# Seven block products for eight in the last feature pairs, and half steps of the attention joined, in a chain of linear attention and two feature layers

## The chip, the core and the metric

The kernel runs on one core of one Trainium2 chip. The metric is the device time of one execution in microseconds; before the change the median of three runs is 912.08 us (911.79 to 914.33).

## What is computed

Linear attention with random features, and then two feature layers on its output, all in float32 or near it (the reference is numpy):

```python
q_p, k_p = (phi(q_s), phi(k_s))           # phi: exp(x @ omega.T - |x|^2/2 - max) / sqrt(m)
kv = np.einsum('bhsm,bhsd->bhmd', k_p, v)
z = np.sum(k_p, axis=2)
num = np.einsum('bhsm,bhmd->bhsd', q_p, kv)
den = np.einsum('bhsm,bhm->bhs', q_p, z)[..., None] + 1e-06
...
h = x @ w_in;  g = h * np.cos(h);  x = g @ w_out                   # first layer
h = x @ w_in;  g = h * np.clip(h + 3.0, 0.0, 6.0) / 6.0;  x = g @ w_out   # second layer
```

There are 4 x 576 = 2304 tokens, 8 heads of 64, 128 random features, a model width of 512 and a feature width of 2048.

## The kernel before

**Order.** The kernel writes down tasks with `add(name, key, engines, function, after, alloc, use)`: a key, a duration per engine, the tasks it comes after, and the ring of buffers it takes a place in. `Plan.order` goes through them with a clock of its own. Each engine that is free takes the ready task with the smallest key (plus the number that `BIAS` holds for its kind), and the instructions are issued in the order that comes out. So keys and durations set the order on each engine; the hardware waits only on the data. Where the plan foresees TensorE idle in the first stretch it puts in matmuls on zeros (`filler`, issued at L1272 and L1281).

**Attention.** 18 chunks of 128 tokens for the keys and 18 for the queries (`chunk`). Each chunk has a projection onto the features (L503, 64 rows of the array), in some chunks a second product for the squared norms (L512), maxima on VectorE (L529) and exponents on ScalarE (L555). Even and odd heads are the halves `hf` 0 and 1. A key chunk adds to the sums `kv` in two tasks, one per half (L570; 64 columns of the array); a query chunk is transposed (L600), divided into a numerator task `num` per half (L613, 64 columns), normalised (L634) and transposed back into `xx` (L648). In the trace each of these float32 matmuls is two records, so that half a numerator has 16.

**First layer, first 4 of 16 feature blocks.** `pair_slot`: plain products, with weights and inputs split into a rounded high part and the rest, three matmuls for one (high by high, low by high, high by low); the input product is L846, the output product L872, 256 columns each.

**The rest: sweeps of two feature pairs.** A pair is 256 features; there are 6 left of the first layer and 8 of the second, numbered j from 0 to 13. A sweep takes two pairs over three blocks of 768 tokens (2 x `NS`). For each pair and block, `quad` makes the first product h = x @ w_in by seven block products in place of eight (L1058), each of 6 matmuls of 384 columns. The seven use sums of blocks: sums of the input (t1 to t4, made in `forms`, kept in DRAM as `xd`) and of the weights (`pair_forms`). Each chain has the banks A, Bk, C, Dk, E. Product 0 goes to A; a seed (ScalarE, L1071) copies A to Bk while product 4 goes to E; then products 1 on A, 5 on Bk (giving u2), a seed of Bk to C, product 6 on Bk (u3), a seed of Bk to Dk, product 2 on C and product 3 on Dk. E is copied out (L401) and added to Bk and C (L1095, L1098).

In the second layer the gate is a ReLU on ScalarE (L1115) and a VectorE step (L1118); then the result is split into a high part (L401, ScalarE) and a low part (L408, VectorE or GpSimd). `units` makes the second product, g @ w_out, as eight plain outputs of 128 rows by 384 tokens, 12 matmuls each (L1196), evicted into `xx` by VectorE (L1223) and stored (L1241). The very last output is cut in two of 192 tokens. Quads have six PSUM banks (`hb`), outputs two (`yb`).

## Time and profile before

| | |
|---|---|
| median of 3 runs | 912.08 us (911.79 to 914.33) |
| the profiled execution | 912.33 us, its span 910.6 us |
| TensorE busy | 902.7 us (99%), 6970 matmuls |
| VectorE / ScalarE / GpSimd busy | 640.7 / 542.1 / 229.7 us |
| granted TensorE clock | 0.999 of full speed |
| matmuls of the second product in sweeps (L1196) | 2028 |

The span is from the first to the last instruction of the one profiled execution; the time of a run is a little longer. A matmul's mean duration in the tables includes its way through the array, which overlaps with the next one, so spacing is read from starts. An engine named as a releaser is the one whose semaphore came last.

### The profile page before, as it was taken

The page shows a single profiled execution, that of the slowest core. Times are in us where ns is not written, and L with a number is a line of the kernel's source. Part 1 is how long each engine was busy: PE and PEld are TensorE (multiplying, and loading weights), DVE is VectorE, ACT ScalarE, POOL GpSimd, SP SyncE. Part 2 cuts the span into 40 slices and gives each one's busy share as a digit, 9 for nine tenths or more (in the row PEclk, how much of TensorE's full clock was granted, in tenths as well). Part 3 has the DMA queues.
Part 4 walks back from the last instruction along what each step waited for, and adds up shares of the span by engine and source line. Part 5 has one row for each costly group of instructions (what it writes and reads, how often), then busy time and mean ns, then how long its engine had stood idle before and what let it go on. Part 6 is the DMA issues. An engine that isn't in the chain of part 4 may idle for free.

```text
span 910.6 us, 17402 instructions
## 1 busy us (share of the span) xinstructions
PE 902.7 (99%) x6970; PEld 882.8 (97%) x6970; DVE 640.7 (70%) x1038; ACT 542.1 (60%) x1084; POOL 229.7 (25%) x174
## 2 busy tenths in 40 slices
PE   9999999999999999999999999999999999999998
PEld 7888999999999999999999999999999999999998
DVE  4886896776679788977668789765676667745442
ACT  7988888985487656656456467654544344434320
POOL 2130313335445433322242433012022002200000
PEclk9999999999999999999999999999999999999999
DMA  8645353423678647741645167522932646153412
GB/s 318 217 143 171 130 196 141 165 73 97 228 298 278 222 144 260 271 174 52 238 136 199 47 254 324 196 93 97 391 136 93 242 157 226 47 199 112 192 54 103
DMA packets 44736, 162.02 MB, mean 178 GB/s; under 512 B 4592, under 2 KB 15984, under 8 KB 40560
## 3 DMA queue, kind: packets, MB, share of 16 engines
q1 hardware_dynamic: 44512, 160.85, 48.9%
q8 instruction: 55, 0.90, 0.4%
q14 instruction: 25, 0.20, 0.1%
q10 hardware_dynamic: 144, 0.07, 0.0%
HBM read 118.43 MB, written 42.47 MB: 177 GB/s over the span
## 4 chain that ended last, share of the span: by engine, by line
PE 95%; DVE 2%; issue 1%; DMA 1%; ACT 1%; SPq 0%; POOL 0%; DVEq 0%; ACTq 0%
PE b L1196 38%; PE b L1058 33%; PE b L846 6%; PE b L872 5%; PE b L503 4%; PE b L570 2%; PE b L613 2%; PE b L600 2%; PE b L512 1%; PE b L648 1%; DMA F<-kT 1%; DVE R L408 0%; PE b L1272 0%; DVE F L529 0%; DVE F L736 0%
## 5 line engine op out<-in xcount | busy, mean ns | idle before, releaser
L408 POOL TENSOR_TENSOR R<-F,R 128x384 fp32r<-128x384 f32 (+3 forms) x103 | 170.8, 1663 | 282.1 <-ACT R L401 248.3
L401 ACT ACTIVATE R<-F 128x768 fp32r<-128x768 f32 (+3 forms) x242 | 174.0, 739 | 101.5 <-PE b L1196 56.5
L1196 PE MATMUL b<-R,R 128*128 128x384 f32 (+1 forms) x1062 | 201.7, 334 | 0.0
L1196 PEld LDWEIGHTS b<-R,R 128*128 128x128 f32 x1062 | 185.1, 188 | 0.0
L1058 PE MATMUL b<-R,R 128*128 128x384 f32 x966 | 183.7, 334 | 0.0
L1196 PE MATMUL b<-R 128*128 128x384 f32 (+1 forms) x966 | 183.3, 334 | 0.0
L1058 PEld LDWEIGHTS b<-R,R 128*128 128x128 f32 x966 | 168.7, 188 | 0.0
L1196 PEld LDWEIGHTS b<-R 128*128 128x128 f32 x966 | 168.4, 188 | 0.0
L1058 PE MATMUL b<-R 128*128 128x384 f32 x798 | 152.8, 334 | 0.0
L1058 PEld LDWEIGHTS b<-R 128*128 128x128 f32 x798 | 139.4, 188 | 0.0
L408 DVE TENSOR_TENSOR R<-F,R 128x384 fp32r<-128x384 f32 (+3 forms) x147 | 128.3, 895 | 11.2 <-ACT R L401 9.2
L1223 DVE SCALAR_TENSOR_TENSOR F<-b,F 128x384 f32<-128x384 f32 (+1 forms) x133 | 73.4, 552 | 87.7 <-PE b L1196 86.8
L1071 ACT ACTIVATE b<-b 128x384 f32<-128x384 f32 x126 | 59.4, 477 | 78.0 <-PE b L1058 77.5
L555 ACT ACTIVATE F<-b,F 128x128 f32<-128x128 f32 x288 | 81.9, 411 | 11.0 <-DVE F L540 10.4
L938 POOL TENSOR_TENSOR F<-F 128x256 f32<-128x256 f32 x40 | 31.3, 797 | 194.7 <-DVE F L736 186.8
L401 ACT ACTIVATE F<-b 128x512 f32<-128x512 f32 (+2 forms) x104 | 55.6, 551 | 30.0 <-PE b L1058 16.1
L529 DVE TENSOR_REDUCE F<-b 128x4 f32<-128x512 f32 x72 | 47.9, 685 | 33.1 <-PE b L512 19.4
L846 PE MATMUL b<-R 128*128 128x256 f32 x432 | 62.1, 290 | 0.0
L872 PE MATMUL b<-R 128*128 128x256 f32 x432 | 58.5, 286 | 0.2 <-ACT F L888 0.2
L846 PEld LDWEIGHTS b<-R 128*128 128x128 f32 x432 | 54.5, 190 | 1.7
L872 PEld LDWEIGHTS b<-R 128*128 128x128 f32 x432 | 54.2, 191 | 0.9 <-ACT F L888 0.4
L503 PE MATMUL b<-F 64*128 64x128 f32 x576 | 42.8, 286 | 0.6 <-DMA F<-kT 0.6
(71 smaller groups left out, 917.2 us busy)
## 6 DMA issues: line engine op xcount, KB each, us to landing
R<-xd SPq DMA_DIRECT2D x77, 768.0 KB, 6.8
F<-w SPq DMA_DIRECT2D x32, 1024.0 KB, 5.3
xd<-R SPq DMA_DIRECT2D x42, 768.0 KB, 4.0
F<-vn SPq DMA_DIRECT2D x18, 260.0 KB, 4.2
F<-qT SPq DMA_DIRECT2D x18, 256.0 KB, 2.8
yy<-F SPq DMA_DIRECT2D x18, 256.0 KB, 2.2
F<-kT SPq DMA_DIRECT2D x17, 256.0 KB, 4.0
F<-qn SPq DMA_DIRECT2D x15, 256.0 KB, 3.8
```

The costliest lines, as they stand in the source:

```text
L401: nc.scalar.activation(out=o, in_=i, func=ACTF.Copy)
L408: (nc.gpsimd if e == "p" else nc.vector).tensor_tensor(out=o, in0=a, in1=b, op=ALU.subtract)
L503: nc.tensor.matmul(out=buf["pj", kind, c, o][:, 128 * i:128 * i + 128], lhsT=buf[X][64 * o:64 * o + 64, 128 * i:128 * i + 128], rhs=omd[64 ...
L529: nc.vector.tensor_reduce(out=buf[MX][:, o:o + 4], in_=pj, axis=AX.X, op=ALU.min)
L555: nc.scalar.activation(out=p[:, o], in_=pj[:, o], func=ACTF.Exp, scale=-1.0, bias=mx[:, b:b + 1])
L846: nc.tensor.matmul(out=o, lhsT=w[:, 128 * kc:128 * kc + 128], rhs=v, start=(kc == 0 and j == 0), stop=(kc == KC - 1 and j == 2), skip_grou ...
L872: nc.tensor.matmul(out=y, lhsT=w[:, o], rhs=v, start=(first and fi == 0 and j == 0 and ec % 2 == 0), stop=(last and fi == 1 and j == 2 and ...
L938: (nc.gpsimd if e == "p" else nc.vector).tensor_tensor(out=st[:, o:o + 256], in0=x, in1=y, op=op)
L1058: nc.tensor.matmul(out=o, lhsT=a, rhs=v, start=first and kc == 0 and q == 0, stop=kc == 1 and q == 2, skip_group_check=True)
L1071: nc.scalar.activation(out=buf[to][:, 0:NS], in_=buf[frm][:, 0:NS], func=ACTF.Copy)
L1196: nc.tensor.matmul(out=o, lhsT=a, rhs=v, start=q == 0 and not seeded, stop=q == 6 * SWEEP - 1, skip_group_check=seeded)
L1223: nc.vector.scalar_tensor_tensor(out=o, in0=y, scalar=r, in1=o if s else buf[YP].bitcast(F32), op0=ALU.mult, op1=ALU.add)
```

## The change

It does four things.

1. For the last two feature pairs (j = 12 and 13, the last sweep; `FAST` = 12) the second product is made by seven block products too (`fast_units`). Its blocks are 256 output rows by 384 tokens, over 128 features of each pair. The 256 rows are done 128 at a time, so each block of tokens has two chains (`e_` 0 and 1) of seven products, of 6 matmuls of 384 columns each (two pairs by three), in banks `fa` to `fe` out of all eight (`h8`). Four evictions per chain add A, Bk, C and Dk to the output, and E is added to two of the four outputs by evictions of its own (`ev0`). The weights' second half becomes seven forms (`wv`) where it had four blocks, and the gated result gets sums t1 to t4 of its own (`gated`: tiles `tt`, then high and low parts in the rings `gs` and `gt`). The last output is not cut in two any more, and each output is stored by itself.
2. The two halves of a key chunk's sums are one task, and so are the two halves of a query chunk's numerator.
3. An exponent of the first half waits for its own maximum alone, where the norms come from TensorE.
4. The plan counts 0.095 us for a change between 128-row, 64-row and 64-column work on TensorE (`T_TURN`), and all keys' constants (`T_P`, `T_LATE`, `BIAS` and others) and some choices of engine (`ENGS`) have other values, so that the order is another one throughout.

The core of the diff:

```diff
-T_P = 37.717
+T_P = 28.537
...
-T_LATE = 36.64
-T_ONE = -48.724
+T_LATE = 56.155
+T_ONE = 70.329
...
-T_K = 2.362
-T_Q = 32.71
+T_K = 2.456
+T_Q = 44.05
...
+FAST = sum(L_PAIRS) - SWEEP
...
+    **{f"wf{i}": spread(*at, 3584, 1) for i, at in enumerate([(R1, 8704), (R2, 0), (R1, 0)])},
+    **{f"wo{i}": spread(*at, 2048, 1) for i, at in enumerate([(R1, 12288), (R2, 3584), (R1, 3584)])},
+    **{f"wv{i}": spread(*at, 3584, 1) for i, at in enumerate([(R1, 12288), (R2, 3584)])},
+    "xf6": spread(R1, 5632, 1536, 2) + spread(R2, 7168, 1536, 4) + spread(R1, 0, 1536, 2),
+    "gs": spread(R1, 16384, 768, 4) + spread(R2, 13312, 768, 2) + spread(R1, 4608, 768, 1),
+    "gt": spread(R1, 19456, 1536, 2) + spread(R2, 14848, 1536, 1) + spread(R1, 3072, 1536, 1),
+    "wg": spread(F1, XX + 5888, 1536, 1) + spread(F1, XX, 1536, 1),
+    "tt": spread(F1, XX + 7424, 768, 1) + spread(F1, XX + 1536, 768, 2) + spread(F1, XX + 4096, 768, 1),
+    "h8": spread(PS, 4, 1, 2) + spread(PS, 0, 1, 4) + spread(PS, 6, 1, 2),
...
+RINGS["gsL"] = RINGS["gs"] + [(a, x, x + 768) for a, lo, hi in RINGS["xf6"] for x in (lo, lo + 768)]
+RINGS["gtL"] = RINGS["gt"] + RINGS["xf6"]
...
+T_TURN = 0.095
...
+                    if e == "t" and t.half not in (None, half):
+                        end, half = end + T_TURN, t.half
...
-        add(P1, k, {"t": 1.0}, proj, ["om"], alloc=pr, use=[X, P0])
+        add(P1, k, {"t": 0.9}, proj, ["om"], alloc=pr, use=[X, P0])
...
-            for hf in range(2):
-                E = ("e", kind, c, hf)
-                for b, r0, r1 in rows(c):
-                    def kv(e, b=b, r0=r0, r1=r1, hf=hf, E=E, first=not kv_parts[b, hf]):
-                        if first:
-                            bank(("kv", b, hf))
-                        p = buf["kv", b, hf]
+            E = [("e", kind, c, hf) for hf in range(2)]
+            for b, r0, r1 in rows(c):
+                first = not kv_parts[b]
+                K0, K1 = ("kv", b, 0), ("kv", b, 1)
+
+                def kv(e, b=b, r0=r0, r1=r1, first=first):
+                    if first:
+                        bank(("kv", b, 1))
+                    for hf in range(2):
                         for h in range(4):
                             for j in (0, 64):
                                 nc.tensor.matmul(
-                                    out=p[j:j + 64, 65 * h:65 * h + 65],
+                                    out=buf["kv", b, hf][j:j + 64, 65 * h:65 * h + 65],
+                                    lhsT=buf[E[hf]][r0:r1, 128 * h + j:128 * h + j + 64],
...
-                    parts = kv_parts[b, hf]
-                    name = ("kv", b, hf) if not parts else ("kv", b, hf, c)
...
-                    parts.append(name)
+                if first:
+                    add(K0, k + 2.9, {"t": 0.01}, lambda e, K0=K0: bank(K0), alloc="kv0", use=E + [V])
+                name = K1 if first else ("kv", b, 1, c)
+                add(name, k + 3, {"t": 0.96}, kv, kv_parts[b][-1:], alloc="kv1" if first else None, use=E + [V, K0] + ([] if first else [K1]))
+                kv_parts[b].append(name)
...
-            def num(e, QT=QT, NUM=NUM, hf=hf):
-                p = bank(NUM)
...
-            add(NUM, k + 4.5 + 0.1 * hf, {"t": 0.58}, num, [("kvs", b, hf) for b, _, _ in rows(c)] + ([("num", c, 0)] if hf else [("tp", c, 1)]), alloc="pt",
-                use=[QT] + [("kvs", b, 0) for b, _, _ in rows(c)])
+            def num(e):
+                bank(("num", c, 1))
+                for hf in range(2):
...
+            if hf == 0:
+                add(NUM, k + 4.5, {"t": 0.01}, lambda e, NUM=NUM: bank(NUM), [("tp", c, 1)], alloc="pt", use=[QT])
+            else:
+                add(NUM, k + 4.6, {"t": 0.96}, num, [("kvs", b, x) for b, _, _ in rows(c) for x in range(2)], alloc="pt",
+                    use=[("qt", c, 0), QT, ("num", c, 0)] + [("kvs", b, 0) for b, _, _ in rows(c)])
...
-    def pair_forms(j):
-        k = w_key(j) + 12.0
...
+    def seven(j, hf, ring):
...
-        made = split("a", WF, FORM_HI, 0, 768, lambda: buf[T0][:, 0:768], [T0], [("low", j, 0)], 0, "wf")
+        made = split("a", WF, 0, 768, lambda: buf[T][:, 0:768], [T], [("low", j, hf)], 0, ring)
...
-        made += split("c", ("wfh", j, "c"), FORM_HI, 768, 1024, lambda: buf[ST], [ST, WF], prev, 0.3)
-        return made, split("o", WO, 1024, 0, 1024, lambda: buf[T1], [T1], [("low", j, 1)], 12, "wo")
+        return made + split("c", (f + "h", j, "c"), 768, 1024, lambda: buf[ST], [ST, WF], prev, 0.3)
+    def pair_forms(j):
+        place = f"{j % 3}"
+        made = seven(j, 0, "wf" + place)
+        if j >= FAST:
+            return made, seven(j, 1, "wv" + place)
...
+            if j >= FAST:
+                gated(n, k, ((("b", A, c11, 5.2, 0, NS), ("r", HS, ("c12", n), 12.1, NS, NP), ("d", Dk, c21, 13.8, 3 * NS, NS))), s * n_p + n_p - 1 == tour.index((s, p)))
+                return
...
+        def gated(n, k, parts, final):
...
+                def relu(e, h=h, o=o, N=N, x=x):
+                    w = tile_of(W, [128, 4 * NS]) if x == "b" else buf[W]
+                    nc.scalar.activation(out=w[:, o:o + N], in_=buf[h][:, 0:N], func=ACTF.Relu, bias=3.0)
...
+                def gg(e, h=h, o=o, N=N):
+                    w = buf[W][:, o:o + N]
+                    nc.vector.scalar_tensor_tensor(out=w, in0=w, scalar=6.0, in1=buf[h][:, 0:N], op0=ALU.min, op1=ALU.mult)
...
+            def t13(e):
+                w = buf[W]
+                sub2(e, tile_of(T1, [128, NP]), w[:, NS:3 * NS], w[:, 0:2 * NS])
...
+            def t2(e):
+                sub2(e, tile_of(T2, [128, NP])[:, 0:NS], buf[W][:, 2 * NS:3 * NS], buf[T1][:, 0:NS])
...
+            def t4(e):
+                sub2(e, buf[T2][:, NS:NP], buf[W][:, 3 * NS:4 * NS], buf[T2][:, 0:NS])
...
+            add(T1, k + 13.0, {"v": 0.96}, t13, [("gg", n, "b"), ("gg", n, "r")], alloc="tt", use=[W])
+            add(T2, k + 13.5, {"v": 0.56}, t2, alloc="tt", use=[W, T1])
+            add(("tu", n), k + 14.5, {"v": 0.56}, t4, [("gg", n, "d")], use=[W, T2])
+            for x, src, o, N, ready, dk in (
+                ("b", W, 0, NS, ("gg", n, "b"), 6.2), ("c", W, 2 * NS, NS, ("gg", n, "r"), 13.0), (0, T1, 0, NP, T1, 13.7), ("d", W, 3 * NS, NS, ("gg", n, "d"), 14.6), (1, T2, 0, NP, ("tu", n), 15.0),
...
+                def hi(e, src=src, o=o, N=N, G=G):
+                    rnd(e, tile_of(G, [128, 2 * N])[:, 0:N], buf[src][:, o:o + N])
+
+                def lo(e, src=src, o=o, N=N, G=G):
+                    sub(e, buf[G][:, N:2 * N], buf[src][:, o:o + N], buf[G][:, 0:N].bitcast(F32))
+
+                add(G, k + dk, {"a": 0.82 if N == NP else 0.52}, hi, [ready] + ([last_g[0]] if last_g[0] else []), alloc=y + far, use=[src])
+                add((y + "l", n, x), k + dk + 0.5, {"v": 0.96 if N == NP else 0.56}, lo, use=[src, G])
+                last_g[0] = G
+
...
+        G_AT = {"b11": ("gs", "b", 0, NS), "b21": ("gs", "d", 0, NS), "b22": ("gs", "c", 0, NS),
+                "t1": ("gt", 0, 0, NP), "t3": ("gt", 0, NS, NP + NS), "t2": ("gt", 1, 0, NP), "t4": ("gt", 1, NS, NP + NS)}
...
+        def fast_units(k_, s, p):
...
+            for e_ in range(2):
...
+                def product(i, bank_of, first, after, alloc=None, e_=e_, k=k, m=m):
...
+                        for q in range(SWEEP):
+                            wv, g = buf["wv", SWEEP * s + q], buf[G[q]]
+                            c0 = 256 * w + 128 * e_
+                            for t, (a, v) in enumerate(((c0, hi), (FORM_HI + c0, hi), (c0, lo))):
+                                nc.tensor.matmul(out=o, lhsT=wv[:, a:a + 128], rhs=g[:, v:v + NS], start=first and q == 0 and t == 0,
+                                                 stop=q == SWEEP - 1 and t == 2, skip_group_check=True)
...
+                    name = bank_of if alloc else ("fp", m, i)
+                    add(name, k + 2.1 * ORDER.index(i), {"t": 1.04}, fn, [(y + "l", n0 + q, z) for q in range(SWEEP)] + [f for q in range(SWEEP) for f in made[SWEEP * s + q][1]] + list(after),
+                        alloc=alloc, use=G + [("wv", SWEEP * s + q) for q in range(SWEEP)] + ([] if alloc else [bank_of]))
...
+                def seed(to, frm, dk, after, k=k):
+                    def fn(e):
+                        bank(to)
+                        nc.scalar.activation(out=buf[to][:, 0:NS], in_=buf[frm][:, 0:NS], func=ACTF.Copy)
+
+                    add(to, k + dk - 10, {"a": 0.5}, fn, after, alloc="h8", use=[frm])
+
+                head = e_ == 0 and p == tour[s * n_p][1]
+                gate = [("ba", n0 + SWEEP - 1)] + ([("y2",) + tour[k_ - 1] + (7,)] if head else [("fa", m - 1)]) + ([("fd", m - 2)] if m - 2 >= 2 * s * n_p else [])
+                product(0, A, True, gate, "h8")
+                seed(Bk, A, 1.1, [A] + ([] if head else [("fd", m - 1)]))
+                product(4, E, True, [A], "h8")
+                c11 = product(1, A, False, [Bk, E])
+                u2 = product(5, Bk, False, [c11])
+                seed(C, Bk, 7.4, [u2])
+                u3 = product(6, Bk, False, [C, u2])
+                seed(Dk, Bk, 9.6, [u3])
+                c12 = product(2, C, False, [u3])
+                c21 = product(3, Dk, False, [c12])
...
+                for u, own, done, dk in ((e_, A, c11, 6.0), (6 + e_, Bk, Dk, 11.0), (4 + e_, C, c12, 12.8), (2 + e_, Dk, c21, 14.9)):
...
+                    def ev(e, b=own, ec=ec, tok=tok):
+                        o = xx[:, ec, tok]
+                        nc.vector.scalar_tensor_tensor(out=o, in0=buf[b][:, 0:NS], scalar=r, in1=o, op0=ALU.mult, op1=ALU.add)
+
+                    def ev0(e, ec=ec, tok=tok, E=E):
+                        o = xx[:, ec, tok]
+                        nc.vector.scalar_tensor_tensor(out=o, in0=buf[E][:, 0:NS], scalar=r, in1=o, op0=ALU.mult, op1=ALU.add)
+
+                    def st(e, ec=ec, tok=tok):
+                        nc.sync.dma_start(out=out[128 * ec:128 * ec + 128, tok], in_=xx[:, ec, tok])
...
+                    if c:
+                        add(("ev0", s, p, u), k + 4.0, {"v": 0.56}, ev0, old, use=[E])
+                        old = [("ev0", s, p, u)]
+                    add(("ev2", s, p, u), k + dk, {"v": 0.56}, ev, [done] + old, use=[own])
+                    add(("st2", p, u), k + dk + 0.5, {"d": 0.4}, st, [("ev2", s, p, u)])
...
-            units(k_, s, p)
+            (fast_units if SWEEP * s >= FAST else units)(k_, s, p)
...
-def _pairs(w_in, w_out, first):
+def _pairs(w_in, w_out, first, fast=0):
...
-    parts = [a[:, 0, 0], a[:, 0, 1], a[:, 1, 1], a[:, 1, 0], o[:, 0], o[:, 1]]
-    return np.ascontiguousarray(np.concatenate(parts, axis=2)[first:]).view(np.uint64)
+    o = [o[:, 0, :, 0:256], o[:, 0, :, 256:512], o[:, 1, :, 0:256], o[:, 1, :, 256:512]]
+    parts = [a[:, 0, 0], a[:, 0, 1], a[:, 1, 1], a[:, 1, 0]]
+    all_ = np.concatenate(parts + o, axis=2)
+    if fast:
+        all_[-fast:] = np.concatenate(parts + [o[0], o[2], o[3], o[1]], axis=2)[-fast:]
+    return np.ascontiguousarray(all_[first:]).view(np.uint64)
...
-        "w2": _pairs(inputs["moe2_w_in"], inputs["moe2_w_out"], 0),
+        "w2": _pairs(inputs["moe2_w_in"], inputs["moe2_w_out"], 0, SWEEP),
```

## Rows read from the trace of the kernel before

**Rows 1.** The page's table of engines: busy time, share of the span, instructions.

```profile
PE 902.7 (99%) x6970; PEld 882.8 (97%) x6970; DVE 640.7 (70%) x1038; ACT 542.1 (60%) x1084; POOL 229.7 (25%) x174
```

**Rows 2.** What TensorE waited for: us in all, times, longest; five in all.

```profile
PE b L648 <- DVE F L634: 2.6, 3, 1.6
...
PE b L872 <- ACT F L888: 0.2, 1, 0.2
```

**Rows 3.** Stretches (from:to, us): busy time of each engine, granted clock, DMA share, GB/s.

```profile
40.00:60.00 20.00, 19.25 (x344) 17.04 (x344) 17.51 (x34) 18.41 (x54) 6.73 (x6) 1.00 0.34 110
...
120.00:140.00 20.00, 20.00 (x226) 18.52 (x226) 17.78 (x41) 17.24 (x36) 4.68 (x4) 1.00 0.50 172
...
300.00:400.00 100.00, 100.00 (x579) 100.00 (x578) 84.06 (x126) 60.55 (x103) 34.71 (x22) 1.00 0.61 217
...
844.00:878.00 34.00, 34.00 (x198) 34.00 (x197) 15.96 (x27) 11.32 (x22) 0.00 (x0) 1.00 0.35 137
```

**Rows 4.** Groups by line and shape: count, busy us, mean ns of one, idle before.

```profile
L401 ACT ACTIVATE R<-F 128x768 fp32r<-128x768 f32 x98 | 81.4, 842 | 33.3 <-PE b L1196 19.1 <-DVE F L1022 8.3 <-DVE F L1148 2.2
L1223 DVE SCALAR_TENSOR_TENSOR F<-b,F 128x384 f32<-128x384 f32 x131 | 72.7, 555 | 86.0 <-PE b L1196 85.1
...
L1118 DVE SCALAR_TENSOR_TENSOR F<-F 128x768 f32<-128x768 f32 x24 | 23.5, 977 | 16.0 <-ACT F L1115 15.9
...
L1272 PE MATMUL b<-F 128*128 128x128 f32 x26 | 4.7, 299 | 0.0
...
L1281 PE MATMUL b<-F 128*128 128x128 f32 x14 | 2.1, 290 | 0.0
```

**Rows 5.** The chain that ended last, in order of time: start us, us, what.

```profile
225.46 2.88 PE b L846 x24
...
419.27 14.56 PE b L1058 x84
```

**Rows 6.** Timeline of the end, all engines: start us, us, engine, line, operation.

```profile
904.79 0.81 PE L1196 MATMUL b<-R 128*128 128x192 f32 x6
...
906.78 0.83 PE L1196 MATMUL b<-R,R 128*128 128x192 f32 x6
907.65 0.36 DVE L1223 SCALAR_TENSOR_TENSOR F<-b,F 128x192 f32<-128x192 f32 x1 [0.98 <-PE b L1196]
```

**Rows 7.** DMA issues of the output: count, KB each, median us to landing.

```profile
yT<-F SPq DMA_DIRECT2D x7, 192.0 KB, 1.9
...
yT<-F SPq DMA_DIRECT2D x2, 96.0 KB, 1.6
```

**Rows 8.** Timeline of one quad: two products, and the seed between them.

```profile
820.55 1.20 PE L1058 MATMUL b<-R 128*128 128x384 f32 x6
820.75 0.47 ACT L1071 ACTIVATE b<-b 128x384 f32<-128x384 f32 x1 [0.69 <-PE b L1058]
```

**Rows 9.** TensorE's timeline in the attention: start us, us, line, tile, count.

```profile
9.30 0.69 PE L570 MATMUL b<-F 128*64 128x65 f32 x16
...
13.12 1.16 PE L570 MATMUL b<-F 128*64 128x65 f32 x32
14.20 1.16 PE L503 MATMUL b<-F 64*128 64x128 f32 x16
...
88.50 0.69 PE L570 MATMUL b<-F 128*64 128x65 f32 x16
...
92.85 0.69 PE L613 MATMUL b<-F 128*64 128x65 f32 x16
93.47 1.70 PE L846 MATMUL b<-R 128*128 128x256 f32 x12
95.10 0.69 PE L613 MATMUL b<-F 128*64 128x65 f32 x16
...
217.71 0.69 PE L613 MATMUL b<-F 128*64 128x65 f32 x16
```

More of the change, by code (lines that the diff above doesn't have):

```diff
@@ L125, in phase @@
     n1 = L_PAIRS[0] * NT // NP
[L126 removed]
+    if x in ("ws", "wt", "clamp", "shift", "sign", "low", "wv", "wvh", "wvl", "wf", "wfh", "wfl", "st", "sum", "wo", "wol"):
         return 0 if name[1] < SWEEP else 1 if name[1] < L_PAIRS[0] else 2
@@ L154, in engines, with halved @@
     return {e: SLOW[kind][e] for e in ENGS.get(f"{kind}{x}", "v")}
-SHARED = ("clamp", "shift", "sign", "low", "wl", "xl", "gl", "wfl", "wol", "st", "sum", "ta", "tb", "xfl", "gl2")
+SHARED = ("clamp", "shift", "sign", "low", "wl", "xl", "gl", "wfl", "wol", "st", "sum", "ta", "tb", "xfl", "gl2", "wvl", "tt", "tu", "gsl", "gtl")
 def shares(name):
     return isinstance(name, tuple) and (name[0] in SHARED or name[0] in ("nr", "gg", "wk2") and name[2] == "r")
+def halved(name):
+    x = name[0] if isinstance(name, tuple) else name
+    if len(name) > 2 and (x == "pj" and not name[3] or x == "kv" and not name[2] or x == "num" and not name[2]):
+        return None
+    return 2 if x in ("kv", "num") else int(x in ("ps", "pj"))
 class Task:
@@ L171, in __init__ @@
         self.shares = shares(name)
+        self.half = halved(name)
 NEVER = 1e9
+T_TURN = 0.095
 class Plan:
@@ L224, in order @@
         lock = [0.0]
+        half = 0
         def can(t, now, e):
@@ L442, in attention_moe_moe2_kernel @@
     last_chunk = {b: ((b + 1) * S - 1) // 128 for b in range(B)}
-    kv_parts = {(b, hf): [] for b in range(B) for hf in range(2)}
+    kv_parts = {b: [] for b in range(B)}
     t_q = T_K * (NCH + N_EARLY)
@@ L761, in attention_moe_moe2_kernel, with pair_weight @@
     pairs = [(w1, i) for i in range(L_PAIRS[0])] + [(w2, i) for i in range(L_PAIRS[1])]
-    for j, (src, i) in enumerate(pairs):
+    def pair_weight(j, hf):
+        src, i = pairs[j]
         gate = [("ba", 3 * j - 5 - j % 2)] if j >= SWEEP else [("in", W_AFTER[j], 3)]
@@ L766, in attention_moe_moe2_kernel @@
                 gate.append(("tb", m, NT // NP - 1, "t4"))
+        weight(src[i, :, 2048 * hf:2048 * hf + 2048], (j, hf), w_key(j) + 12.0 * hf, gate, "ws2")
+    for j in range(FAST):
         for hf in range(2):
-            weight(src[i, :, 2048 * hf:2048 * hf + 2048], (j, hf), w_key(j) + 12.0 * hf, gate, "ws2")
+            pair_weight(j, hf)
+    for hf in range(2):
+        for j in range(FAST, len(pairs)):
+            pair_weight(j, hf)
     last_x = [None]
@@ L939, in sums, with hi, lo @@
             return fn
[L941 removed]
+        prev = [("low", j, hf)]
         for i in range(4):
[L943 to L944 removed]
+            name = ST if i == 0 else ("sum", j, i, hf)
+            add(name, k + 0.2 + 0.01 * i, engines("sum", phase(WF)), sums(i), prev, alloc=None if i else "st", use=[T] + ([ST] if i else []))
             prev = [name]
[L946 to L947 removed]
+        return made + split("c", (f + "h", j, "c"), 768, 1024, lambda: buf[ST], [ST, WF], prev, 0.3)
[4 more added lines that the diff above has]
+            return made, seven(j, 1, "wv" + place)
+        k = w_key(j) + 24.0
+        WO, T = ("wo", j), ("wt", j, 1)
+        def hi(e):
+            rnd(e, tile_of(WO, [128, 2048])[:, 0:1024], buf[T])
+        def lo(e):
+            sub(e, buf[WO][:, 1024:2048], buf[T], buf[WO][:, 0:1024].bitcast(F32))
+        add(WO, k, {"a": 1.03}, hi, [("low", j, 1)], alloc="wo" + place, use=[T])
+        add(("wol", j), k + 0.1, engines("wol", phase(("wf", j))), lo, use=[T, WO])
+        return made, [WO, ("wol", j)]
     def stage():
@@ L1267, in filler @@
     def filler(last):
-        for hf in range(2):
-            for b in range(B):
-                if last.get(("kv", b, hf)) and not last.get((kv_parts[b, hf][-1])):
-                    return lambda: nc.tensor.matmul(out=buf["kv", b, hf][:, 0:FILL], lhsT=zero[:, 0:128], rhs=zero[:, 0:FILL], start=False, stop=False, skip_group_check=True)
+        for b in range(B):
+                if last.get(("kv", b, 1)) and not last.get(kv_parts[b][-1]):
+                    return lambda: nc.tensor.matmul(out=buf["kv", b, 1][:, 0:FILL], lhsT=zero[:, 0:128], rhs=zero[:, 0:FILL], start=False, stop=False, skip_group_check=True)
         for b in range(N_A):
```

100 lines of the change are left out of this document (62 added, 38 removed).

## The prediction

> **What bounds the kernel.** I read the table of engines first. TensorE is busy in 99% of the 910.6 us span; no other engine passes 70% [rows 1]. A busy TensorE need not be a full one, so the list of its waits comes next: five waits in the whole execution, from 2.6 us in all for the attention's last transpose down to 0.2 us [rows 2]. The table of stretches then shows that this holds everywhere: from 120 to 140 us and from 300 to 400 us TensorE has no gap, at a granted clock of 1.00, the 2.4 GHz level, while VectorE and ScalarE are 61 to 89% busy [rows 3]. Only the first 90 us or so are looser: 19.25 of 20 us between 40 and 60, with ScalarE at 18.4 [rows 3], and part of that is matmuls on zeros (L1272 and L1281), which the plan puts where it foresees TensorE idle: 4.7 and 2.1 us [rows 4]. So the time is the sum of what TensorE does. A matmul taken away is a gain of its own spacing, unless it leaves a hole; work added on the other engines costs nothing until TensorE waits for it.
>
> The spacing comes from the chain of work in order of time. 84 matmuls of 384 columns take 14.56 us, 173.3 ns each, and 24 of 256 columns take 2.88 us, 120 ns each [rows 5].
> By the Trainium skill ("TensorE: Matmul & The Clock Gate", Back-to-back issue gap) a warm matmul of N columns takes N/2.4 + 2.5 ns, 162.5 ns here; the trace's 173.3 is 7% longer, and by the page term 1 below would be 5.85 us in place of 6.24, the whole sum 0.4 us smaller.
>
> **1. Seven products for eight: -6.24 us.** The last sweep has three token blocks. For each, the second product now takes 96 matmuls: 8 outputs of 12. After, two halves of 7 products of 2 pairs of 3 matmuls: 84. That is 36 matmuls fewer, times 173.3 ns. The sweep's first product is as before.
>
> **2. The last output is no longer cut in two: -0.1 us.** Now its 24 matmuls of 192 columns start at 904.79, and the last ends at 906.78 + 0.83 = 907.61 [rows 6]. Twelve of 384 columns would end after 11 x 0.173 + 0.33 = 2.24 us, at 907.03: 0.58 us earlier. But the last eviction is of 384 columns (0.555 us [rows 4], not 0.36 [rows 6]), and the last store is of 192 KB, 1.9 us to land, not of 96 KB, 1.6 us [rows 7]: 0.58 - 0.20 - 0.3.
>
> **3. The seeds: +0.7 us.** In a chain of seven products, ScalarE copies a bank into the next (the seed) between the product on bank B that makes u2 and the product that makes u3, which then overwrites B's sum. In before, the other kind of work fills the hole. TensorE's next group starts at 820.55, the copy of what it left starts at 820.75 and takes 0.47 us [rows 8]; with a hand-off as short as the 0.04 us between the last matmul's end and the last eviction [rows 6], the hole is 0.20 + 0.47 + 0.04 = 0.7 us. The seed of B is covered by product E (6 x 173 = 1.04 us), that of D by c12. In the last sweep there are 6 new chains and 6 old; five of the new ones have quad products or the next chain's first products (A and E) to put into the hole. The very last has nothing: its predecessor's c12 and c21 have lower keys and are gone by then. So 0 to 6 x 0.7 = 4.3 us; I take one.
>
> **4. More work for VectorE and ScalarE in the last sweep: +0.7 us.** Per quad VectorE did two additions, three gates and three low parts: with 0.555 us for 384 columns and 0.98 for 768 [rows 4], 5.3 us; two quads and 8 evictions make 15.0 us per block, and the stretch from 844 to 878 shows 15.96 [rows 3]. Now three differences of G (2.1 us) and two more low parts (1.5) come to each quad, and four evictions of E (2.2) to each block (with six seeds, 18 readings of a bank where 8 were): 24.4 us against TensorE's 2 x 7.28 + 14.56 = 29.1. ScalarE gets two more roundings per quad (1.4) and six seeds (2.9): some 17 us. Both still fit. What can hurt is when, not how much. Four gt slots hold one block's sums; the next block's wait until the chain before lets them go. After u3 lets T1 go, two roundings of 0.84 [rows 4] and a low part of 0.98 follow, some 3 us with hand-offs; c12, c21 and the next A, 3.1 us, run meanwhile. So a slot costs nothing if VectorE is free. It is fullest at the sweep's first chain: three low parts of T (2.9), the late weights' two (2.2) and four of 384 columns (2.2), 7.4 us, under up to 7.3 to 14.6 us of quad products. Between nothing and 7.4 - 3.1 = 4.3 us for a block (7.4 where even A waits); I take 0.7, one more seed's hole, nearest to a trace in which such roundings have held up TensorE nowhere after 300 us [rows 2, 3]. The banks (8, where quads had 6 and outputs 2) belong here: two chains at 3 to 4 live banks each fit.
>
> The late weights take seven forms, not four: 0.84 us more on ScalarE, 0.98 on VectorE and four sums on GpSimd for each of two pairs, under 30 us of quads; if late, the first chain waits, which the 7.4 holds. Stores go from 17 to 24, issued by a queue that orders them behind loads already made: nothing, and the last is term 2.
>
> **5. The numerator's halves in one step: -4.8 us.** TensorE's own timeline shows what a change of tile shape costs. Half a numerator (16 recorded matmuls, 128*64) takes 0.62 us until the next start, at 92.85; the 12 input matmuls of 128*128 between the halves take 1.63 [rows 9], against 12 x 120 ns = 1.44 in an unbroken run [rows 5]: 0.19 for the split. Two halves that stand together, of the keys' product, which has the same shape, take 1.08 (13.12 to 14.20 [rows 9]), against 2 x 0.615 = 1.23 apart: 0.15. One merge removes both: 0.34. From 92.85 to 217.71 all 14 chunks have their halves apart, with full-size matmuls between [rows 9]: 4.8 us. The first four chunks' halves stand beside the keys' (no gain). The merged step waits for both rounded halves; TensorE has input and output products to do meanwhile, in a stretch without a gap. Bounds 14 x 0.15 = 2.1 and 4.8; the timeline shows both parts, so the upper.
>
> **6. The keys' halves: -0.9 us.** 17 halves stand alone, from 9.30 to 88.50 [rows 9]. Some 8 pairs at 0.34 would be 2.7 us. But this is the stretch with zeros and waits, where ScalarE sets the pace: what is saved may come back as waiting. Bounds 0 and 2.7; I take a third, as the waits and zeros cover most of it. Exponents that start after their own half's maximum only shorten a latency here; so 0. New keys without new work can't change a TensorE sum that has no gaps: 0 beyond 90 us.
>
> **Sum**: -6.24 - 0.10 + 0.7 + 0.7 - 4.8 - 0.9 = -10.6. The profiled execution took 912.33 (its span and 1.7 us around it), 0.25 above the median of 912.08. 912.33 - 10.6 = 901.7, or 901.5 by the median: I say **901.7**.
>
> **Rivals.**
> *A. The merges don't pay.* The attention stretch is set by ScalarE after all (17.24 of 20 us at 120 to 140 [rows 3]); fewer switches then become waits. Against it: TensorE has no gap there. Terms 5 and 6 gone: 907.4.
> *B. Holes in the last sweep, worse than before.* VectorE, 84% taken, comes late with the sums of G, and TensorE has run out of quad products. The first block's chain also needs the late weights for its product A, so its whole 7.4 us lie bare; the other two lose 4.3 each: 16.0 us for the 0.7, 917.0. It decides from (10.6 + 0.7)/3 = 3.8 us a block; a later block alone gives 905.3, the first alone 908.4, the first with another 912.7. For it: four gt slots, and 24.4 of 29.1. Against: an interleaving that leaves no gap in the same sweep now [rows 3].
> By the Trainium skill ("TensorEngine Tiling (Array Packing)", PSUM Bottleneck) a faster TensorE leaves the emptying of PSUM as it was, which may then become the bottleneck; that speaks for B, and no run here shows it yet.
> *C. More than the sum.* The keys' merges pay in full (-1.8), no seed is bare (-0.7), VectorE is never late (-0.7): 898.5.
>
> **Chances and numbers.** The forecast, 899.5 to 904.5: 0.57. C: 0.14. A, whole or in good part: 0.14. B in one block: 0.09, in two: 0.03, in full: 0.03. A measurement here can tell about 0.3%, 2.7 us, from no change: faster is below 909.3, slower above 914.8. So B in two blocks is the case of no change, with a part of B in the first block under a bare seed; B in full is the slower one: faster 0.92, same 0.05, slower 0.03. The range reaches from C to just short of A's full price, 898.5 to 907.2, leaving out the tail of C and most of B.
>
> **What would show it.** 7 x 6 x 6 = 252 matmuls of the new second product where 288 + 12 stood; groups of 6 in the last 29 us with one hole of about 0.7 us before a u3. L613's successor in runs of 32 from 90 us on, and the start of the dense feature work some 5 us earlier. Wrong if TensorE's waits in the last 100 us exceed 3 us, naming VectorE's low parts or ScalarE's copies, or if waits and zeros in the first 90 us grow by what the merges save.

## The result, and the profile after

The changed kernel takes 902.47 us (median of 4 runs, 901.17 to 903.72), the kernel before 913.03 us on the same chip (4 runs, 911.79 to 914.33): a ratio of 0.9884 (95% interval [0.9862, 0.9906]; the brackets below are such intervals), 10.6 us less. The profiled execution of the changed kernel took 903.72, the longest of its four; its span is 901.9 us. The same program run again on another chip (y0_again) gave 902.16 (901.37 to 902.91).

The table of engines of the changed kernel, beside [rows 1]:

```profile
PE 894.5 (99%) x6958; PEld 879.4 (97%) x6958; DVE 680.0 (75%) x1090; ACT 554.1 (61%) x1108; POOL 213.9 (24%) x181
```

TensorE is as full as before and has less to do; VectorE has 39 us more and ScalarE 12. What TensorE waited for, beside [rows 2]:

```profile
PE b L445 <- DVE F L442: 1.2, 1, 1.2
PE b L678 <- DVE F L664: 0.7, 2, 0.4
PE b L1301 <- ACT b L1312: 0.6, 1, 0.6
PE b L527 <- ACT F L579: 0.5, 1, 0.5
```

The queries' transpose (L648 before, L678 now) waits less, 0.7 for 2.6 us. The third line is new: the new second product waiting for a seed, once. Lines by shape, beside [rows 4], show the changed work:

```profile
L1301 PE MATMUL b<-R,R 128*128 128x384 f32 x150 | 29.2, 335 | 0.6 <-ACT b L1312 0.6
L640 PE MATMUL b<-F 128*64 128x65 f32 x576 | 20.7, 224 | 0.0
L1301 PE MATMUL b<-R 128*128 128x384 f32 x102 | 20.4, 334 | 0.0
...
L1457 PE MATMUL b<-F 128*128 128x128 f32 x50 | 7.3, 283 | 0.0
L1466 PE MATMUL b<-F 128*128 128x128 f32 x24 | 3.8, 288 | 0.0
```

The new second product is 150 + 102 = 252 matmuls, as forecast. The zeros (L1457, L1466; two more at L1460) are 76 where 40 stood. The stretches that answer to [rows 3]:

```profile
120.00:140.00 20.00, 20.00 (x225) 19.09 (x224) 17.73 (x37) 17.41 (x37) 6.17 (x5) 1.00 0.60 198
844.00:878.00 34.00, 34.00 (x198) 34.00 (x197) 27.14 (x50) 18.13 (x35) 0.00 (x0) 1.00 0.23 84
841.00:894.00 53.00, 53.00 (x308) 53.00 (x306) 41.22 (x74) 25.37 (x49) 0.00 (x0) 1.00 0.28 103
```

In the last sweep VectorE goes from 15.96 to 27.14 us in 34, and TensorE has no gap up to 894 us.

### The profile page after: what moved, and what is told of

Read it like the earlier page. It is cut to its first block, busy times and chain, and to the rows that moved or that the text cites. A ratio compares the mean times of both kernels' runs of the same rounds, so it can differ in the third digit from the quotient of the medians.

```text
span 901.9 us, 17464 instructions
## 1 busy us (share of the span) xinstructions
PE 894.5 (99%) x6958; PEld 879.4 (97%) x6958; DVE 680.0 (75%) x1090; ACT 554.1 (61%) x1108; POOL 213.9 (24%) x181
## 4 chain that ended last, share of the span: by engine, by line
PE 97%; DVE 1%; DMA 1%; ACT 0%; issue 0%; SPq 0%; DVEq 0%; ACTq 0%
PE b L1114 34%; PE b L1382 33%; PE b L909 6%; PE b L883 6%; PE b L1301 5%; PE b L527 4%; PE b L596 2%; PE b L640 2%; PE b L626 2%; PE b L536 2%; PE b L678 1%; PE b L1457 1%; DMA F<-kT 1%; DVE F L553 0%; ACT F L579 0%; PE b L1466 0%
## 5 line engine op out<-in xcount | busy, mean ns | idle before, releaser
L425 ACT ACTIVATE R<-F 128x384 fp32r<-128x384 f32 (+3 forms) x252 | 179.6, 732 | 86.2 <-PE b L1382 45.2
L432 POOL TENSOR_TENSOR R<-F,R 128x384 fp32r<-128x384 f32 (+3 forms) x82 | 130.6, 1596 | 293.9 <-ACT R L425 264.1
L1114 PE MATMUL b<-R,R 128*128 128x384 f32 x966 | 182.8, 334 | 0.0
L1382 PE MATMUL b<-R,R 128*128 128x384 f32 x960 | 179.6, 334 | 0.0
L432 DVE TENSOR_TENSOR R<-F,R 128x768 fp32r<-128x768 f32 (+3 forms) x182 | 158.2, 890 | 18.5 <-ACT R L425 17.0
L1114 PEld LDWEIGHTS b<-R,R 128*128 128x128 f32 x966 | 168.5, 188 | 0.0
L1382 PEld LDWEIGHTS b<-R,R 128*128 128x128 f32 x960 | 167.6, 188 | 0.0
L1114 PE MATMUL b<-R 128*128 128x384 f32 x798 | 151.2, 334 | 0.0
L1382 PE MATMUL b<-R 128*128 128x384 f32 x768 | 145.8, 334 | 0.0
L1114 PEld LDWEIGHTS b<-R 128*128 128x128 f32 x798 | 139.3, 188 | 0.0
L1382 PEld LDWEIGHTS b<-R 128*128 128x128 f32 x768 | 134.3, 188 | 0.0
L977 POOL TENSOR_TENSOR F<-F 128x256 f32<-128x256 f32 x64 | 50.9, 812 | 234.9 <-DVE F L766 226.5
L1409 DVE SCALAR_TENSOR_TENSOR F<-b,F 128x384 f32<-128x384 f32 x108 | 59.8, 554 | 48.2 <-PE b L1382 47.6
L579 ACT ACTIVATE F<-b,F 128x128 f32<-128x128 f32 x288 | 80.5, 399 | 11.9 <-DVE F L564 5.7
L425 ACT ACTIVATE F<-b 128x512 f32<-128x512 f32 (+2 forms) x104 | 55.2, 549 | 38.6 <-PE b L1114 18.7
L883 PE MATMUL b<-R 128*128 128x256 f32 x432 | 58.9, 288 | 0.3 <-DVE F L848 0.3
L909 PE MATMUL b<-R 128*128 128x256 f32 x432 | 58.2, 286 | 0.0
L883 PEld LDWEIGHTS b<-R 128*128 128x128 f32 x432 | 53.7, 190 | 1.4 <-DVE F L848 0.5
L909 PEld LDWEIGHTS b<-R 128*128 128x128 f32 x432 | 54.0, 191 | 0.5
```

The lines of the kernel that those rows point to most:

```text
L425: nc.scalar.activation(out=o, in_=i, func=ACTF.Copy)
L432: (nc.gpsimd if e == "p" else nc.vector).tensor_tensor(out=o, in0=a, in1=b, op=ALU.subtract)
L579: nc.scalar.activation(out=p[:, o], in_=pj[:, o], func=ACTF.Exp, scale=-1.0, bias=mx[:, b:b + 1])
L883: nc.tensor.matmul(out=o, lhsT=w[:, 128 * kc:128 * kc + 128], rhs=v, start=(kc == 0 and j == 0), stop=(kc == KC - 1 and j == 2), skip_grou ...
L909: nc.tensor.matmul(out=y, lhsT=w[:, o], rhs=v, start=(first and fi == 0 and j == 0 and ec % 2 == 0), stop=(last and fi == 1 and j == 2 and ...
L977: (nc.gpsimd if e == "p" else nc.vector).tensor_tensor(out=st[:, o:o + 256], in0=x, in1=y, op=op)
```

## Where the time went

I added up, over TensorE's whole timeline, the distances from each start to the next, by line, for the kernel before, the changed kernel and y0_again. Up to the last output matmul of the attention (266.23 us before) the changed kernel gains 3.4 us in its profiled execution and 4.8 in y0_again; from there to the end of the last matmul 5.9 and 5.3. After it, the longer eviction and store cost 0.6.

The 1.5 us between the two executions of one program lie in the first microseconds. In the changed kernel's profile (first four lines) and in y0_again's (the last two, its code one line further down):

```profile
4.05 2.08 PE L527 MATMUL b<-F 64*128 64x128 f32 x16
...
8.31 2.92 PE L536 MATMUL b<-F 64*128 64x128 f32 x32
11.16 1.38 PE L1466 MATMUL b<-F 128*128 128x128 f32 x10
12.47 1.16 PE L527 MATMUL b<-F 64*128 64x128 f32 x16
```

```profile
4.04 3.29 PE L528 MATMUL b<-F 64*128 64x128 f32 x32
9.05 1.38 PE L1467 MATMUL b<-F 128*128 128x128 f32 x10
```

Sixteen projection matmuls take 2.08 us at the start and 1.16 later, about half: in one execution TensorE reaches its full pace while the halves at 8.31 run, in the other during the projections at 4.04. The first zeros start at 11.16 or at 9.05. The column of the granted clock says 1.00 here in both, but it counts the time for which the trace has no entry as full speed. The list of entries that each trace keeps, from which that column is made, begins with an entry at full speed (the 2.4 GHz level) at 10.34 us in the changed kernel's profile, at 6.67 in y0_again's and at 4.91 in that of the kernel before. Up to that entry one recorded projection or norm matmul starts 106 ns or more after the one before it (mean of two), mostly 107; behind it the median is 56. So it is in 13 of the 14 traces; in z1_old_keys the entry comes at 4.17, ahead of nearly all of them. The pace before the entry is that of the 1.2 GHz level, half of the other; that the clock was there is worked out from the pace, as no entry names the level. TensorE had been at work since 1.19 us in all three. Why the rise comes at another time in each isn't shown.

This matters for the comparison. x1_eight, y1_hole, y3_low_twice and z5_small_low_twice below issue the same matmuls in the same order up to the end of the attention. Their lists begin at 4.70 to 5.50 us, close to the 4.91 of the kernel before, and their profiles gain 4.7 to 5.3 us there. The 3.4 is short because of its late rise; about 5 is the better figure. No difference of some 2 us between two profiles is to be read without looking at this place.

The attention, in the changed kernel, beside [rows 9]:

```profile
103.22 1.15 PE L640 MATMUL b<-F 128*64 128x65 f32 x32
104.31 3.13 PE L883 MATMUL b<-R 128*128 128x256 f32 x24
...
113.11 1.15 PE L640 MATMUL b<-F 128*64 128x65 f32 x32
114.19 2.06 PE L909 MATMUL b<-R 128*128 128x256 f32 x15
```

A whole numerator takes 1.09 us to the next start, where two halves took 2 x 0.62, and the 24 matmuls behind it stand in one run.

The end of the last sweep:

```profile
892.60 1.73 PE L1301 MATMUL b<-R,R 128*128 128x384 f32 x9
...
894.36 0.47 ACT L1312 ACTIVATE b<-b 128x384 f32<-128x384 f32 x1 [3.31 <-PE b L1301]
894.89 3.42 PE L1301 MATMUL b<-R,R 128*128 128x384 f32 x18 [0.56 <-ACT b L1312]
```

Nine matmuls of 173.3 ns from 892.60 end their turn at 894.16; u3 starts at 894.89, when the seed of C is copied: a hole of 0.73 us, 0.56 of it listed as a wait. The other five new chains show none.

## Experiments

Each is the changed kernel with the edit shown or named, and compared with the kernel before on its own chip (912.80 to 912.86 there). Differences are taken to the changed kernel's 902.47 and y0_again's 902.16. Where a kernel is a line longer, its lines stand one further down.

**y0_again: the changed kernel once more.**

> The changed kernel once more, unaltered but for an empty line, as the measure for the runs beside it: 902.5 us, 0.9884 of the kernel before. Its first projections show whether the clock's rise, at about 11 us in the first profile, comes at the same place; if it comes at about 5 us as in the kernel before, the profiled time is some 2 us lower, 901.5 to 902.

902.16 us, 0.9883 [0.9869, 0.9896].

**x1_eight: eight products in the last sweep again, all else as changed.**

```diff
-FAST = sum(L_PAIRS) - SWEEP
+FAST = sum(L_PAIRS)
...
-        "w2": _pairs(inputs["moe2_w_in"], inputs["moe2_w_out"], 0, SWEEP),
+        "w2": _pairs(inputs["moe2_w_in"], inputs["moe2_w_out"], 0),
```

> The changed kernel with the last sweep's second product made by eight block products again, cut last output included; all else, the order up to the last sweep too, as changed. My sum: 36 matmuls (6.24 us), the last output's cut (0.1) come back, the bare seed (0.7) and the 0.7 for VectorE go: 5 us above the changed kernel's 902.5, so 907.5, a gain of 5.5 us left to the attention. Rival (the block products gave all, the attention gave its savings back as zeros and waits): 912. Rival (the attention gave all, the last sweep's holes ate the 6.24): 902.5.

907.78 us (907.13 to 908.11), 0.9943 [0.993, 0.9956]. The block products are worth 5.3 to 5.6 us: terms 1 to 4 said 4.94. The other half of the gain, 5.1 us, is there without them.

**x2_num_apart: the numerator's second half one TensorE task later, for the 14 later chunks, in the same order.**

```diff
-            t.fn(e)
+            if apart(x):
+                t.fn(e, part=0)
+                late = (t.fn, followers(t))
...
+                late[0](e, part=1)
```

> The changed kernel in its own order, but from query chunk 4 on the second half of the numerator is issued one TensorE task later, so that the two halves stand apart in 14 chunks, 12 of them with full-size matmuls between. By 0.34 us a split with full-size work between and 0.15 where the projection stands there: 12 x 0.34 + 2 x 0.15 = 4.4 us slower, 906.9. If only the halves' own starts count (0.15): 2.1 us, 904.6. Rival (ScalarE sets the pace there): no change, 902.5, with the time taken from waits and zeros.

909.52 us (908.88 to 910.1), 0.9964 [0.9952, 0.9976]: 7.1 to 7.4 slower, where the price of the switches was 4.4. By the sums over the timeline the numerator's own matmuls take 2.1 us more (14 x 0.15) and the input and output products between the halves 2.4 (14 x 0.17): 4.5 together, the price as I had it. The rest is waiting; first its list of waits, then its timeline:

```profile
PE b L679 <- DVE F L665: 3.5, 5, 1.8
```

```profile
93.48 0.69 PE L641 MATMUL b<-F 128*64 128x65 f32 x16
94.10 0.98 PE L884 MATMUL b<-R 128*128 128x256 f32 x6
95.01 0.69 PE L641 MATMUL b<-F 128*64 128x65 f32 x16
95.62 0.94 PE L1467 MATMUL b<-F 128*128 128x128 f32 x6
97.43 0.66 PE L679 MATMUL b<-F 128*128 128x128 f32 x4 [0.87 <-DVE F L665]
```

The transpose L679 comes after VectorE's work on the numerator. With six matmuls between the halves the numerator is done later and the transpose waits 3.5 us in all, for 0.7.

**x3_kv_apart: the keys' second half later.** Some of the delayed halves read exponents that the next chunk's had replaced, so both its data and its waits are altered.

> The changed kernel in its own order, but the second half of each key chunk's sums is issued one TensorE task later (20 splits in the first 90 us). My term of 0.9 us for the merge says that two thirds of what switches cost there is covered by waits: 0.9 us slower, 903.4. Were TensorE the bound there, some 15 splits of 0.15 to 0.34 would make 3 to 5 us, 906.5. Rival (the stretch is ScalarE's): 0, 902.5.

908.56 us (906.51 to 913.12), 0.9957 [0.9944, 0.997]. I take nothing from it; y2_kv_apart asks the same with the buffers respected.

**y2_kv_apart: the keys' halves apart, 16 of 20, each before its buffer is taken over.**

```diff
+        def apart(x):
+            return isinstance(x, tuple) and x[0] == "kv" and (len(x) == 4 or x[2] == 1)
...
+            if late and (e == "t" or x in late[1] or taken_over(t, late[2])):
```

> The changed kernel in its own order, with the second half of the key chunks' sums one TensorE task later, unless a buffer that it reads is taken first (16 of 20 stand apart). My theory, two thirds covered by waits and zeros: 1.4 us slower, 903.9. Rival, TensorE is the bound in the first 90 us too: 16 x 0.15 and some 10 runs of projections cut at 0.19, 4.3 us slower, 906.8. Rival, the stretch is ScalarE's: 902.5.

904.47 us (904.21 to 904.69), 0.9909 [0.9894, 0.9924]: 2.3 slower than y0_again on the same chip. The keys' matmuls take 2.1 us more, and TensorE's waits are 1.1 less. Of the full price, 4.3, about half came through, where term 6 counted on a third. In the trace the keys' matmuls stand in 30 runs for the changed kernel's 16; the kernel before has 28, so that its merge, at this price, is worth about 12/14 of 2.3, or 2.0 us: between the 0.9 I took and the 2.7 that I had as the upper end.

**x4_no_zeros: no matmuls on zeros.**

> The changed kernel in its own order without the matmuls on zeros (76 recorded, 10.4 us of TensorE's timeline; before the change 40 and 6.1). If they stand where TensorE would wait anyway: same time within 1 us, 902.5, and about 10 us of waits in their place. If they hold up work, because the plan's idle time is longer than the real one: up to 4 us faster, 898.5. If the granted clock falls in the holes: slower, with a clock under 1.00 in the first 90 us.

901.25 us (900.8 to 902.27), 0.9875 [0.9862, 0.9888]: about 1 less, which the intervals don't part from nothing. The 76 zeros stand for 10.4 us of TensorE's timeline; without them its gaps grow by 5.0 to 5.5 us, the longest of them for the exponents (L579):

```profile
PE b L527 <- ACT F L579: 2.8, 4, 1.0
PE b L678 <- DVE F L664: 1.3, 2, 1.1
```

The zeros cost little: of 10.4 us only about 1 comes back. Half turns into waits, and some 3 us into longer distances between the matmuls that are left in the attention, most of them projections (1.9 us). The granted clock stays at 0.998 to 1.00 in all four runs, so its fall, the third case, did not come.

**y1_hole: the last-but-one chain's last product (c21) held back until the last chain's u2.**

```diff
-                c21 = product(3, Dk, False, [c12])
+                c21 = product(3, Dk, False, [c12] + ([("fp", m + 1, 5)] if m == 2 * len(tour) - 2 else []))
```

> The changed kernel with the last product of the last chain but one (c21, 6 matmuls, 1.04 us) held back until the last chain's u2, so that it stands in the one bare seed. If that hole of 0.7 us is a loss of its own: 0.5 to 0.7 us faster, 901.9, and no wait of TensorE for the seed. If the hole only moves (before c11, which waits for two seeds): same, 902.5.

901.73 us (901.66 to 901.87), 0.9878 [0.9865, 0.9892]: 0.4 less than y0_again, which its runs alone can't tell from nothing. Its timeline can: the last 33 matmuls stand in one run, no wait for a seed is left in its list, and the time from the attention's end to the last matmul's is 634.9 us, for 635.6 in the changed kernel's profile and 636.2 in y0_again's.

```profile
890.33 5.89 PE L1301 MATMUL b<-R,R 128*128 128x384 f32 x33
```

**y3_low_twice: every low part of G in the last sweep made twice; z5_small_low_twice: only those of 384 columns.** The output stays as it was; VectorE gets more to do.

```diff
-                    sub(e, buf[G][:, N:2 * N], buf[src][:, o:o + N], buf[G][:, 0:N].bitcast(F32))
+                    for _ in range(2):
+                        sub(e, buf[G][:, N:2 * N], buf[src][:, o:o + N], buf[G][:, 0:N].bitcast(F32))
```

In z5 the new line is `for _ in range(2 if N == NS else 1):`.

> The changed kernel with every low part of the last sweep's G made twice on VectorE (the same values; 7.3 us more a block, 31.7 in place of 24.4 us against TensorE's 29.1). If VectorE is only short of its limit there, as I reckon: TensorE waits for the difference of 2.6 us a block and what piles up at the end, 5 to 9 us slower, 909. If the chains had no slack: all 3 x 7.3 = 22 us, 924. If there is much more slack than I think: under 2 us, 904.

> The changed kernel with only the low parts of 384 columns of the last sweep's G made twice on VectorE: 3 x 0.56 us a quad, 10 us in all, where all low parts twice were 21.6 us and cost 14.4. If VectorE has a fixed slack of about 7 us there: 2 to 4 us slower, 905. If what comes through is a share of two thirds: 6.7 us slower, 909. If the large low parts alone were what hurt (they come last before a product): under 1 us, 902.5.

y3: 916.6 us (916.09 to 917.42), 1.0041 [1.0028, 1.0053], 14.4 more than y0_again. z5: 904.76 (904.41 to 905.75), 0.9916 [0.9903, 0.993], 2.6 more. VectorE's low parts by shape, in the changed kernel, in y3 and in z5:

```profile
L432 DVE TENSOR_TENSOR R<-F,R 128x768 fp32r<-128x768 f32 x80 | 79.9, 1010 | 7.4 <-ACT R L425 7.3
L432 DVE TENSOR_TENSOR R<-F,R 128x384 fp32r<-128x384 f32 x58 | 33.7, 589 | 5.3 <-ACT R L425 5.3
```

```profile
L432 DVE TENSOR_TENSOR R<-F,R 128x768 fp32r<-128x768 f32 x92 | 91.5, 1004 | 7.7 <-ACT R L425 6.5
L432 DVE TENSOR_TENSOR R<-F,R 128x384 fp32r<-128x384 f32 x76 | 46.0, 611 | 5.5 <-ACT R L425 4.9
```

```profile
L432 DVE TENSOR_TENSOR R<-F,R 128x384 fp32r<-128x384 f32 x76 | 44.2, 587 | 5.5 <-ACT R L425 4.9
```

TensorE's new waits, in y3 and in z5:

```profile
PE b L1114 <- ACT b L1127: 3.4, 3, 1.4
PE b L1302 <- DVE R L432: 2.4, 3, 1.0
PE b L1302 <- ACT b L1313: 2.1, 4, 1.2
PE b L1114 <- DVE F L1337: 1.6, 1, 1.6
```

```profile
PE b L1114 <- ACT b L1127: 1.1, 1, 1.1
```

y3 added 11.6 + 12.3 = 23.9 us and the time grew by 14.4, well past the 5 to 9 of my expectation; z5 added 10.5 and it grew by 2.6, as a fixed slack has it. In both, 8 to 9.5 us went under cover and the rest came out nearly whole: about 3 us for each of the last sweep's three blocks, if they share it evenly. So rival B's holes appear once VectorE has that much more to do; in y3 they make the kernel slower than before, with the waits that B named (low parts and seeds) and one for an eviction that gives a bank back (L1337).

**z1_old_keys: the changed kernel's tasks with the keys and choices of engine of before.**

```diff
-T_P = 28.537
+T_P = 37.717
...
-BIAS = {"sqnk": -149.2, "rd": 167.0, ...}
+BIAS = {"sqnk": -251.0, "rd": 202.7, ...}
```

> The changed kernel with the keys' constants and choices of engine of the kernel before (new kinds of tasks have no offset): the new products and joint steps in an order that no one fitted to them. I priced the new order at nothing: then 902.2 to 903.5, with the attention's 4.8 us and the products' 5 us both there. Rival, the order carries part of it: in the attention fewer changes of tile shape, in the last sweep the holes of my rival B; 906 to 915, with waits named after VectorE's low parts or the seeds after 800 us, or more changes of tile shape before 240 us.

**z2_both_maxima: the first half's exponents wait for both maxima, as before; the plan orders anew by the changed kernel's keys.**

```diff
-                [(("mx", kind, c, 1) if hf else MX) if on_pe else ("b2",) + u] + exp_after + ...
+                [("mx", kind, c, 1) if on_pe else ("b2",) + u] + exp_after + ...
```

> The changed kernel with the first half's exponents waiting for both halves' maxima again. The plan makes another order from it. I priced this part at 0: 902.2, within 1 us. If the earlier exponents shorten the first 90 us: 1 to 3 us slower, with more waits and zeros before 90 us.

z1: 967.19 us (963.86 to 968.57), 1.0582 [1.0563, 1.0601]. z2: 949.71 (948.26 to 951.29), 1.0408 [1.0393, 1.0422]. Both are far outside all that I had expected. First z1's waits, then the row of the granted clock of z2's page and z2's timeline:

```profile
PE b L1114 <- ACT R L425: 19.8, 1, 19.8
PE b L1114 <- ACT b L1127: 7.1, 5, 2.8
```

```profile
PEclk9999999999999999999999968999999999999999
```

```profile
544.75 5.36 PE L1382 MATMUL b<-R,R 128*128 128x384 f32 x30
...
566.74 1.23 DVE L766 SCALAR_TENSOR_TENSOR F<-F 128x1024 uint32<-128x1024 uint32 x1
...
568.06 2.52 ACT L425 ACTIVATE R<-F 128x1024 fp32r<-128x1024 f32 x3 [4.17 <-DVE F L766]
...
569.90 1.01 PE L1114 MATMUL b<-R,R 128*128 128x384 f32 x2 [19.78 <-ACT R L425]
```

In both the largest loss is one hole of 19.8 us where the second layer starts: its weights, decoded on VectorE (to L766) and rounded on ScalarE (L425), come after TensorE has run out of work; in z2 the page's slice that holds most of it has a mean granted clock of 6 tenths and the next of 8, and z2's list of entries has the 1.2 GHz level from 554.7 to 578.6 us, from within the hole to past its end. Neither kernel of [rows 2] or of the list after has such a wait. In all, TensorE waits 41 us more in z1 than in y0_again and 35 more in z2. So z2 can't say what the earlier exponents are worth: its edit set a new order off, and the loss of 47 us covers it. z1 shows that the old keys don't serve the changed set of tasks. The new products themselves suffer little from them: 3 of z1's 44 us of waits stand after 850 us.

**z4_hole_no_zeros: y1 and x4 together.**

> The changed kernel with the last seed's hole filled (as y1_hole) and without the matmuls on zeros (as x4_no_zeros). If both small gains are real and add: 900.6, 0.9868 of the kernel before. If the zeros' gain was chance: 901.7.

900.02 us (899.35 to 900.68), 0.9863 [0.9849, 0.9876]. All four runs lie below all eight of the changed program (901.17 to 903.72), by 2.1 to 2.5 at the medians: 12.8 below the kernel before. It beats both kernels, though chips differ and the step is near what can be told.

## Why the prediction was right

It said 901.7 us, in 898.5 to 907.2; 902.47 was measured. TensorE's spacing set the time before and sets it now.

**Terms 1 to 4 (-4.94; measured 5.3 to 5.6 by x1_eight).** The 252 matmuls and the one bare seed, 0.7 forecast and 0.73 seen, before a u3 of the very last chain, came as worked out; the end after the last matmul cost 0.6 (2.99 to 3.59 us) where 0.5 stood. VectorE's lateness, 0.7, did not come: no other wait is listed in the last sweep. Its slack was mis-sized all the same: 29.1 - 24.4 = 4.7 us a block by arithmetic, about 3 by y3 and z5. Busy time subtracted from a bound was not all usable; that this is because the low parts are due at set moments fits y3's waits, but wasn't tested.

**Term 5 (-4.8).** The price of a split, 0.34, held: 4.5 us for 14 by x2_num_apart. The 2.6 to 2.9 that x2 loses beyond it are the numerator's latency: its transposes wait 3.5 us, for 0.7, and 3.3 of that behind 90 us, in the split chunks. I would not add that to what the merge gained against the kernel before. There the halves stood apart in the same chunks, and of the 2.6 us of [rows 2] 2.3 stand in two early ones, 0.25 behind 90 us:

```profile
45.42 0.66 PE L648 MATMUL b<-F 128*128 128x128 f32 x4 [0.74 <-DVE F L634]
...
63.58 0.66 PE L648 MATMUL b<-F 128*128 128x128 f32 x4 [1.56 <-DVE F L634]
...
172.10 0.66 PE L648 MATMUL b<-F 128*128 128x128 f32 x4 [0.25 <-DVE F L634]
```

An order made with the halves apart covers the latency; x2's was made for joined ones. So 7.1 to 7.4 is what the joined step is worth in this order, and 4.5 is the part that the sum was about. What the sum did miss is where the halves stood; the next paragraph but one has it.

**Term 6 (-0.9).** Too small as a price: about 2.0 by y2_kv_apart. The count behind it was short as well: the keys' matmuls go from 28 runs to 16, so that the merge takes 12 away, where I had some 8. But the sign that I had named against it, waits and zeros that grow, was there too: 34 zeros before 90 us became 64, 5.2 us became 8.6, and with 1.7 to 2.0 us less of waits the two together grew by 1.5 to 1.8, as much as the keys' own matmuls saved (1.7). The first stretch about gave the merge's own saving back, dressed as zeros, as rival A said of it. After 90 us A was wrong.

**The sum of 5 and 6 was -5.7; the profiles show -3.4 and -4.8** up to the end of the attention, and -4.7 to -5.3 where the clock rises about as early as before. In y0_again: numerators -2.1, input and output products -1.3, keys -1.7, query transposes (L600 before, L626 now) -2.4, zeros +4.3, projections and norms -0.5, other waits of this part -1.3. The transposes' share was not in my sum. In the kernel before a half of the numerator starts right behind a query's transposes 17 times, in the changed kernel never. Four transposes in front of a numerator, before, and in front of an input product, now:

```profile
118.49 0.60 PE L600 MATMUL b<-F 128*128 128x128 f32 x4
119.02 0.69 PE L613 MATMUL b<-F 128*64 128x65 f32 x16
```

```profile
108.05 0.60 PE L626 MATMUL b<-F 128*128 128x128 f32 x4
108.40 0.96 PE L883 MATMUL b<-R 128*128 128x256 f32 x6
```

They take 0.53 us to the next start and 0.35. By the medians over the attention the change into the numerator costs 0.17 us behind a transpose (0.20 to the next start for 0.03) and 0.09 behind an input or output product (0.21 for 0.12). A merge took away the first kind, and I had priced the second: 17 x 0.08 = 1.4 us more. z1_old_keys, with the merges and the keys of before, has no numerator right behind these transposes either, so that this goes with the merge and not with the new keys. The changes of tile shape as such fall from 157 to 106 up to 240 us, and nearly all of that is the merges: with the numerators apart there are 132, with the keys apart 127. Too little for the merges stood against too little for the zeros; that these nearly cancelled, and not the terms alone, makes 901.7 come so close. That part is luck.

**"New keys without new work: 0 beyond 90 us"** held, for this pair of orders, as far as the changes of shape tell: from 90 to 240 us they fall by 29, and 26 of these are the numerators' halves. As a statement on keys it fails: z1 loses 65 us by keys and choices of engine alone, z2 47 by one altered dependence and the order that came of it. It holds between two orders of which both leave TensorE no gap, and that was known of one only.

**Open:** what the earlier exponents are worth by themselves, why TensorE's clock rises at another time in each execution, and how the new keys fare without the merges: x2 and y2 put the halves apart one kind at a time, in an order made for joined ones.

## What to carry to other kernels

Where one engine is full, price a removed step by its distance to the next start, and a joined step by both boundaries that it removes: its own and that of the work which really stands next to it; then look who waits for its end: in an order that was made for the joined step, that was more than half as much again. An order from a list of keys is a part of the kernel: test an edit inside the order as it stands, since one made anew can cost more than the edit is worth. The slack that busy times leave on a second engine is to be measured by doubling some of its work; here about two thirds of it could be used.
